# Transposes of a half's feed-forward output made between the next half's key projection tiles, in place of behind them

## The chip, the cores and the metric

The kernel runs on one core of one Trainium2 chip, as a single program. The metric is the device time of one execution in microseconds (us), taken as the median of several runs; lower is better. The engines are named as in the profile: PE is the matrix engine, DVE the vector engine, ACT the scalar engine, POOL the general-purpose engine and SP the engine that issues most DMAs. Each runs its own queue of instructions in order and waits for the others on semaphores.

## The reference

Three blocks follow each other, in float32, for 4 batches of 576 positions:

```python
scores = scale * np.matmul(q, k.transpose(0, 1, 3, 2))        # 8 heads of 64
thresh = np.max(scores, axis=-1, keepdims=True) - tau
attn   = softmax of the scores that reach thresh;  x = attn @ v
xk = mu_k * x + (1.0 - mu_k) * x_prev                         # x_prev: x one position earlier
xr = mu_r * x + (1.0 - mu_r) * x_prev
k = np.maximum(xk @ w_k, 0.0)                                 # 512 -> 1024
v = k * k @ w_v                                               # 1024 -> 512
x = 1.0 / (1.0 + np.exp(-(xr @ w_r))) * v
u = x + real(fft over positions and channels of x)
un = layer norm of u;  out = u + np.maximum(un @ w_ch1, 0.0) @ w_ch2
```

The change touches the second block, the feed-forward, alone.

## The kernel before, in words

The attention of the 16 pairs of heads is cut into 144 steps. From the fifth pair on, the feed-forward runs beside it as a stream: a Python generator, `ffn_stream`, that emits a piece of work, yields its cost and is resumed as attention steps leave credit. What the stream has left when attention ends runs in a second stage, beside the Fourier transform (`fft_fold`, `fft_one`, `fft_two`, on tiles `f`, `fz`, `fa`, `fb`), the first norms (`un`, `ut`) and the conversion of the last block's weights (`wbits`, `cA`, `cB`). The last block (tiles `c1ps`, `c2ps`) follows.

The stream walks over 4 batches with 2 halves of 288 positions each. A half consists of

- K: eight key projection tiles `kps`, 12 matmuls each. ACT evicts each (`relu`, its square, a copy) and POOL makes a low part;
- R: four tiles `rps` of 12 matmuls from `xh`, `xl` and `wr`, evicted by ACT with a tanh into the tile `tg`;
- V: four tiles `vps` of 24 matmuls, which DVE multiplies into `tg`;
- the output, `xt_out`: three tiles `xn` (128, 128 and 32 positions). PE transposes `tg` with four instructions for each, ACT copies the result into a tile `xnat`, and ACT's DMA queue writes that to the tensor `xd`, from which the Fourier transform reads later.

A half's `xt_out` is not run at its own end. It is kept, and the next half runs it after its K and before its R. So it is run behind K in seven of the eight halves; the last half's own output comes at the very end of the stream.

Three pools matter. `kps`, `rps`, `vps`, `xn` and attention's `av` take turns in two PSUM banks (function `bank`). `xnat` has one buffer while attention runs and afterwards shares four buffers, named `o`, with `un` and other tiles. `xh` and `xl`, the operands of K, are in the second stage also the operands of R: function `build_xs` fills them anew once K has read them. While attention runs, and for the very last half, R has buffers of its own and is prepared during K.

The order on each engine is made by a scheduler that plans the emitted instructions by costs of its own. It keeps what each must wait for, but may move work of one part past work of another, so the order written in the kernel is not the one on the engine.

Of the kernel before, what the change touches and what calls it, by code (L numbers as in the profile page):

```python
# [1 line left out]

# [1 line left out]

# [24 lines left out]
def tile_kernel(ctx: ExitStack, tc: tile.TileContext, a):  # L29
# [87 lines left out]
    def bank(shape, name):  # L117
        if psm is None:
            if P['AVR'] == 0:
                return pst.tile(shape, F32, tag="t", name=name)  # L120
            if not avq:
                t = pss.tile([128, 2, 512], F32, tag="s", name="avs")
                avq.extend([t[:, 0, 0:HS], t[:, 1, 0:HS]])
            return avq.pop(0)
        while len(pending) >= 2:
            pending.pop(0)()
        return psm.tile(shape, F32, tag="m", name=name)
# [3 lines left out]
    def settle():  # L131
        go, second[:] = list(second), []
        for f in go:
            f()
        while pending:
            pending.pop(0)()
# [262 lines left out]
    def proj(ps, w, x, m, width, nk):  # L399
        for k in range(nk):  # L400
            wh, wl = (t_[:, k * width + 128 * m:k * width + 128 * m + 128] for t_ in w)
            pe.matmul(ps, wh, x[0][k], start=(k == 0), stop=False)  # L402
            pe.matmul(ps, wh, x[1][k], start=False, stop=False)  # L403
            pe.matmul(ps, wl, x[0][k], start=False, stop=(k == nk - 1))  # L404
# [37 lines left out]
    def ffn_stream():  # L442
        fp = ffn["pool"]
        xt_out = None
        for b in range(B):
            for half in range(2):
                if half == 0:
                    while xdone[P['XH'] == 0] < NPAIR * (b + 1):
                        yield 0
                    xs = build_xs(b, half, 0)  # L450
                while builds:
                    yield 0
                xs_r = build_xs(b, half, 1) if state['at'] or (b, half) == (B - 1, 1) else None
                k2 = [fp.tile([128, 8, HS], F32R, tag=f"k2{i}", name=f"k2{i}") for i in range(2)]
                for f in range(8):
                    ps = bank([128, HS], "kps")
                    proj(ps, wk[f // 4], xs, f % 4, 512, 4)

                    def post(f=f, ps=ps, k2=k2, b=b):
                        r = fp.tile([128, HS], F32, tag="relu", bufs=2, name="relu")  # L460
                        m = P['RQ'][f]
                        if m in (1, 4):
                            dve.tensor_scalar(r, ps, 0.0, None, op0=ALU.max)
                        else:
                            with tc.high_priority(offset=400 if last else 0):
                                act.activation(r, ps, AF.Relu)
                        if m == 2:
                            pool.tensor_tensor(r, r, r, op=ALU.mult)
                        elif m == 5:
                            dve.tensor_tensor(r, r, r, op=ALU.mult)  # L470
                        elif m not in (1, 3):
                            act.activation(r, r, AF.Square)

                        def post2():
                            if m in (1, 3):
                                act.activation(k2[0][:, f, :], r, AF.Square)
                                pool.tensor_tensor(r, r, r, op=ALU.mult)
                            else:
                                act.activation(k2[0][:, f, :], r, AF.Copy)
                            eng = dve if b == B - 1 and f % 4 < P['K2'] else pool  # L480
                            eng.tensor_tensor(k2[1][:, f, :], r, k2[0][:, f, :].bitcast(F32), op=ALU.subtract)

                        second.append(post2)

                    pending.append(post)
                    if f == 3 and (b, half) == (B - 1, 1):
                        ffn["k_done"] = 1
                    yield 1.48
                if b == B - 1 and half == 1:
                    ffn["k_done"] = 2  # L490
                xs_r = xs_r or build_xs(b, half, 1)
                if xt_out:
                    yield from xt_out()
                while builds:
                    yield 0
                if half == 0:
                    while xdone[1] < NPAIR * (b + 1):
                        yield 0
                    xs = build_xs(b, 1, 0)
                for _ in state['late']:  # L500
                    pass
                t = fp.tile([128, 4, HS], F32, tag="t", name="tg")
                for m in range(4):
                    ps = bank([128, HS], "rps")
                    proj(ps, wr, xs_r, m, D, 4)

                    def post(m=m, ps=ps, half=half, t=t):
                        o = t[:, m, ::-1] if half else t[:, m, :]
                        with tc.high_priority(offset=400 if last else 0):
                            act.activation(o, ps, AF.Tanh, scale=0.5)  # L510

                    pending.append(post)
                    yield 1.48
                settle()
                settle()
                if b == B - 1 and half == 1:
                    ffn["r_done"] = True
                for m in range(4):
                    ps = bank([128, HS], "vps")
                    for k in range(8):  # L520
                        c = k * D + 128 * m
                        pe.matmul(ps, wv[0][:, c:c + 128], k2[0][:, k, :], start=(k == 0), stop=False)  # L522
                        pe.matmul(ps, wv[0][:, c:c + 128], k2[1][:, k, :], start=False, stop=False)  # L523
                        pe.matmul(ps, wv[1][:, c:c + 128], k2[0][:, k, :], start=False, stop=(k == 7))  # L524

                    def post(m=m, ps=ps, half=half, t=t):
                        v = ps[:, ::-1] if half else ps
                        with tc.high_priority(offset=400 if last else 0):
                            dve.scalar_tensor_tensor(t[:, m, :], t[:, m, :], 1.0, v, op0=ALU.add, op1=ALU.mult)  # L529

                    pending.append(post)
                    yield 2.95

                def xt_out(b=b, half=half, t=t):
                    settle()
                    for t0 in (0, 128, 256):
                        tn = min(128, HS - t0)
                        ps = bank([128, D], "xn")
                        for m in range(4):
                            pe.transpose(ps[:tn, 128 * m:128 * (m + 1)], t[:, m, t0:t0 + tn], ident)  # L540

                        def post(t0=t0, tn=tn, ps=ps):
                            n = fp.tile([128, D], F32, tag="xn", name="xnat") if last is None else last.tile([128, D], F32, tag="o", bufs=4, name="xnat")
                            if P['XN'] >> (t0 // 128) & 1:
                                dve.tensor_scalar(n[:tn], ps[:tn], 0.5, None, op0=ALU.mult)
                            else:
                                with tc.high_priority(offset=400 if last else 0):
                                    act.activation(n[:tn], ps[:tn], AF.Copy, scale=0.5)
                            r0 = half * (HS + 1) + t0
                            act.dma_start(xd[b][r0:r0 + tn, :], n[:tn])  # L550
                            if half and t0 == 256:
                                act.dma_start(xd[b][HS:HS + 1, :], n[tn - 1:tn])

                        pending.append(post)
                        yield 0.45
                    written[b] += 1

        yield from xt_out()
# [653 lines left out]
```

## Time and profile before

| | us |
|---|---|
| median of 3 runs | 1078.95 |
| lowest, highest | 1077.89, 1082.51 |
| the profiled execution | 1083.47 |
| its span, first to last instruction | 1081.7 |
| PE busy in the span | 1019.9 |

The span lies 1.8 us inside the profiled execution's own time, and that execution is 4.5 us above the median. The stretches that matter are attention with the stream (to about 522 us), the second stage (to about 641 us) and the last block (to the end). An `xn` group begins at 227.7, 297.9, 365.7, 434.5, 503.3, 554.6 and 603.5 us, and the last one, which stays where it is, at 636.8 us.

### The profile page before, as it was taken

To read this page: it belongs to the slowest core of one execution; us is meant where nothing else is said; L and a number is where in the kernel's file an instruction comes from. 1 tells how busy PE (TensorE), PEld (TensorE's weight loads), DVE (VectorE), ACT (ScalarE), POOL (GpSimd) and SP (SyncE) were. 2 spreads that over 40 slices of the span, in tenths; PEclk is the share of its full clock that TensorE was granted. 3 is DMA by queue.
4 is the path that set the end of the run, shared out by engine and by line. 5 is a ranking of instruction groups with operands and counts; after the bars stand their busy time and mean duration, and the time that the engine had idled before them with its cause. 6 is when DMAs were issued, how large, how long until landed. Compare 5 with 4: busy or idle time off the path is not lost.

```text
span 1081.7 us, 18932 instructions
## 1 busy us (share of the span) xinstructions
PE 1019.9 (94%) x6933; PEld 897.4 (83%) x6933; DVE 671.7 (62%) x1797; ACT 518.0 (48%) x1211; POOL 367.8 (34%) x472
## 2 busy tenths in 40 slices
PE   5888889999999999999999899999999999999998
PEld 4555668988889889888899789898898898999997
DVE  6889888667686675765357878556448465222322
ACT  4768676585776757757165645233223122111111
POOL 1555777455673554734233100000014133010000
PEclk9989889999999999999999899999999999999999
DMA  6432421111122111200623565535336435232221
GB/s 233 148 112 75 133 90 59 37 58 59 60 69 60 58 37 60 69 14 23 185 65 103 175 201 183 160 111 193 121 114 187 152 128 174 78 103 93 98 98 59
DMA packets 45526, 114.54 MB, mean 106 GB/s; under 512 B 6208, under 2 KB 6629, under 8 KB 45433
## 3 DMA queue, kind: packets, MB, share of 16 engines
q1 hardware_dynamic: 27920, 74.43, 21.3%
q10 hardware_dynamic: 12200, 22.17, 6.7%
q0 software_dynamic: 5312, 16.72, 4.3%
q8 instruction: 55, 0.90, 0.3%
q14 instruction: 39, 0.31, 0.1%
HBM read 84.98 MB, written 28.32 MB: 105 GB/s over the span
## 4 chain that ended last, share of the span: by engine, by line
PE 65%; DVE 10%; DMA 6%; ACT 5%; issue 3%; POOL 3%; ACTq 0%; DVEq 0%; SPq 0%
PE av L382 5%; PE c1ps L971 5%; PE c1ps L972 5%; PE c1ps L973 5%; PE c2ps L984 5%; PE c2ps L986 5%; PE c2ps L985 5%; PE s L221 4%; DMA wraw<-in_w_ch 3%; PE t L323 3%; PE kps L402 2%; PE kps L404 2%; PE kps L403 2%; PE vps L522 2%; PE vps L523 2%
## 5 line engine op out<-in xcount | busy, mean ns | idle before, releaser
L977 DVE SCALAR_TENSOR_TENSOR hl<-c1ps,hh 128x256 fp32r<-128x256 f32 x144 | 60.7, 422 | 172.5 <-ACT hh L976 172.2
L976 ACT ACTIVATE hh<-c1ps 128x256 fp32r<-128x256 f32 x144 | 55.0, 382 | 224.5 <-PE c1ps L973 221.1
L261 DVE TENSOR_REDUCE small<-s 128x1 f32<-128x576 f32 x144 | 106.8, 752 | 53.7 <-PE s L221 40.4
L1009 POOL DMA_DIRECT2D ud<-u x54 | 29.5, 546 | 288.1 <-DVE u L1008 256.9
L284 POOL TENSOR_SCALAR e<-e,small 128x576 f32<-128x576 f32 x112 | 92.2, 828 | 100.1 <-DVE small L629 84.8
L276 DVE SCALAR_TENSOR_TENSOR e<-s,small,e 128x576 f32<-128x576 f32 x128 | 102.7, 812 | 25.0 <-ACT e L272 23.5
L272 ACT ACTIVATE e<-s,small 128x576 f32<-128x576 f32 x128 | 93.4, 743 | 32.1 <-DVE small L261 29.7
L323 PE MATMUL t<-ident,e 128*128 128x128 f32 x512 | 81.8, 277 | 10.5 <-POOL e L284 3.3
L326 ACT ACTIVATE pt<-t 128x512 f32<-128x512 f32 x128 | 74.6, 599 | 24.7 <-PE t L323 24.4
L971 PE MATMUL c1ps<-ut,cA 128*128 128x256 f32 x288 | 81.7, 284 | 2.9 <-ACT ut L962 1.8
L971 PE MATMUL c1ps<-ut,cB 128*128 128x256 f32 x288 | 81.2, 282 | 0.0
L972 PE MATMUL c1ps<-ut,cA 128*128 128x256 f32 x288 | 81.2, 282 | 0.0
L972 PE MATMUL c1ps<-ut,cB 128*128 128x256 f32 x288 | 81.0, 281 | 0.0
L973 PE MATMUL c1ps<-ut,cA 128*128 128x256 f32 x288 | 81.0, 281 | 0.0
L973 PE MATMUL c1ps<-ut,cB 128*128 128x256 f32 x288 | 80.9, 281 | 0.0
L402 PE MATMUL kps<-xh,wk 128*128 128x288 f32 x256 | 78.8, 308 | 1.5 <-DVE tg L529 1.2
L323 PEld LDWEIGHTS t<-ident,e 128*128 128x128 f32 x512 | 61.1, 142 | 21.0 <-POOL e L284 6.2
L404 PE MATMUL kps<-xh,wk 128*128 128x288 f32 x256 | 77.2, 302 | 0.0
L403 PE MATMUL kps<-xl,wk 128*128 128x288 f32 x256 | 77.1, 301 | 0.0
L522 PE MATMUL vps<-k,wv 128*128 128x288 f32 x256 | 76.8, 305 | 0.0
L523 PE MATMUL vps<-k,wv 128*128 128x288 f32 x256 | 76.4, 302 | 0.0
L524 PE MATMUL vps<-k,wv 128*128 128x288 f32 x256 | 75.4, 300 | 0.0
(246 smaller groups left out, 3041.4 us busy)
## 6 DMA issues: line engine op xcount, KB each, us to landing
u<-ud SPq DMA_DIRECT2D x36, 512.0 KB, 5.7
wraw<-in_w_ch ACTq DMA_DIRECT2D x64, 256.0 KB, 3.1
rawqk<-in_qk SPq DMA_DIRECT2D x24, 608.0 KB, 3.8
ud<-u POOLq DMA_DIRECT2D x54, 256.0 KB, 2.5
v<-in_v SPq DMA_DIRECT2D x16, 320.0 KB, 3.0
un<-ud SPq DMA_DIRECT2D x18, 256.0 KB, 3.6
out<-u SPq DMA_DIRECT2D x18, 256.0 KB, 2.1
wraw<-in_w_k SPq DMA_DIRECT2D x8, 512.0 KB, 3.9
```

Of the source, the lines that this page charges most:

```text
L261: dve.tensor_reduce(st[:, 0:1], sps[n][:, :, 0:HS], axis=AX.XY, op=ALU.max, negate=True)
L272: act.activation(two(eview(n)), sps[n][:, :, 0:HS], AF.Exp, bias=st[:, 0:1])
L276: dve.scalar_tensor_tensor(e, sps[n][:, :, 0:HS], st[:, 1:2], e, op0=ALU.is_ge, op1=ALU.mult, accum_out=st[:, 2:3])
L323: pe.transpose(t[:, k, :], e[:, o + 128 * k:o + 128 * (k + 1)], ident)
L402: pe.matmul(ps, wh, x[0][k], start=(k == 0), stop=False)
L403: pe.matmul(ps, wh, x[1][k], start=False, stop=False)
L404: pe.matmul(ps, wl, x[0][k], start=False, stop=(k == nk - 1))
L522: pe.matmul(ps, wv[0][:, c:c + 128], k2[0][:, k, :], start=(k == 0), stop=False)
L523: pe.matmul(ps, wv[0][:, c:c + 128], k2[1][:, k, :], start=False, stop=False)
L971: pe.matmul(ps, wh, ut[0][:, k, :], start=(k == 0), stop=False)
L972: pe.matmul(ps, wh, ut[1][:, k, :], start=False, stop=False)
L973: pe.matmul(ps, wl, ut[0][:, k, :], start=False, stop=(k == 3))
```

## The change

The generator that makes the three `xn` tiles is created before K. One of its tiles is taken after each of K's tiles 1, 3 and 5 (counted from 0); what is left of it runs after K. The call between K and R is gone.

```diff
+from itertools import islice
...
                 xs_r = build_xs(b, half, 1) if state['at'] or (b, half) == (B - 1, 1) else None
+                turned = xt_out() if xt_out else iter(())
...
                     yield 1.48
+                    if f in (1, 3, 5):
+                        yield from islice(turned, 1)
+                yield from turned
                 if b == B - 1 and half == 1:
                     ffn["k_done"] = 2
                 xs_r = xs_r or build_xs(b, half, 1)
-                if xt_out:
-                    yield from xt_out()
                 while builds:
                     yield 0
```

The number of instructions on each engine is the same before and after, kind by kind. Source lines are higher by 1 to 5 in the changed kernel.

On PE, where K of the half in the stretch from 434 us ends, with attention's scores (`s`) and transposes (`t`, `tm`) around it, the kernel before has:

```order
L404 MATMUL kps_5066<-xh_4676,wk11_87 128x288
L221 MATMUL s_5148<-kh_4800,q_4804 128x288 x2
L221 MATMUL s_5148<-kl_4801,q_4804 128x288 x2
L540 MATMUL xn_5084<-ident_76,tg_4251 128x128 x4
L221 MATMUL s_5210<-kh_4544,q_4635 128x288 x2
L221 MATMUL s_5210<-kl_4545,q_4635 128x288 x2
L540 MATMUL xn_5089<-ident_76,tg_4251 128x128 x4
L540 MATMUL xn_5124<-ident_76,tg_4251 32x128 x4
L343 MATMUL tm_5225<-ident_76,em_5097 128x128 x4
```

The three `xn` tiles stand in a row there, with R behind them. In the changed kernel PE passes from the last K tile of the same half (`kps_5091`) to R without anything between:

```order
L404 MATMUL kps_5091<-xl_4677,wk10_86 128x288
L405 MATMUL kps_5091<-xh_4676,wk11_87 128x288
L403 MATMUL rps_5134<-xh_4742,wr0_90 128x288
L404 MATMUL rps_5134<-xl_4743,wr0_90 128x288
L405 MATMUL rps_5134<-xh_4742,wr1_91 128x288
```

The `xn` tiles have moved up between K tiles. The first of them now stands on PE between K's second tile (`kps_4759`) and its third (`kps_4830`):

```order
L405 MATMUL kps_4759<-xh_4676,wk01_85 128x288
L324 MATMUL t_4815<-ident_76,e_4679 128x128 x4
L324 MATMUL t_4873<-ident_76,e_4679 128x128 x4
L543 MATMUL xn_4778<-ident_76,tg_4249 128x128 x4
L222 MATMUL s_4907<-kh_4795,q_4799 128x288 x2
L222 MATMUL s_4907<-kl_4796,q_4799 128x288 x2
L403 MATMUL kps_4830<-xh_4676,wk00_84 128x288
```

Of the 21 moved tiles 20 have other work of attention or of the transform beside them in this way. One has not: the second of the half that follows attention stands directly between two K tiles.

On PE, in that half (the `xn` group at 554.6 us), the kernel before comes from K through 5.6 us of transform and `xn` work, and then to R, tile after tile:

```order
L811 MATMUL fz_6676<-tc2_6213,G1_6523 1x258
L820 MATMUL fb_6694<-ts2_6214,H1_6525 128x256
L402 MATMUL rps_6648<-xh_6564,wr0_90 128x288
L403 MATMUL rps_6648<-xl_6565,wr0_90 128x288
L404 MATMUL rps_6648<-xh_6564,wr1_91 128x288
```

In the changed kernel 16 transform matmuls are left between K's last tile and R (7 of `f`, 3 of `fb`, 6 of `fz`), and PE makes the first two R tiles (`rps_6691`, `rps_6741`) in turns:

```order
L814 MATMUL fz_6639<-tc2_6213,G1_6500 1x258
L823 MATMUL fb_6657<-ts2_6214,H1_6502 128x256
L403 MATMUL rps_6691<-xh_6623,wr0_90 128x288
L403 MATMUL rps_6741<-xh_6623,wr0_90 128x288
L404 MATMUL rps_6691<-xl_6624,wr0_90 128x288
L405 MATMUL rps_6691<-xh_6623,wr1_91 128x288
```

After 12 matmuls of R come 7 of the transform (`fz`, `fb`), two of R, 7 of `fa`, six of R and 7 of `fa`; the rest of R follows.

On ACT, in the last half (the `xn` group at 603.5 us), the kernel before evicts the three `xn` tiles together, between steps of the transform (`fee`, `fdd`):

```order
L834 ACTIVATE fee_7475<-zr_7457 1x257
L548 ACTIVATE xnat_7267<-xn_7239 128x512
L833 ACTIVATE fdd_7474<-zr_7457 1x257
L550 DMA xd3_66<-xnat_7267 128x512
L548 ACTIVATE xnat_7270<-xn_7262 128x512
L548 ACTIVATE xnat_7348<-xn_7313 32x512
```

The changed kernel evicts the first two among K's tiles, and the third (`xnat_7248`) behind K's last one (`kps_7284`):

```order
L468 ACTIVATE relu_7300<-kps_7284 128x288
L55 DMA wraw_7353<-in_w_ch2 128x512
L551 ACTIVATE xnat_7248<-xn_7239 32x512
L474 ACTIVATE relu_7300<-relu_7300 128x288
L553 DMA xd3_66<-xnat_7248 32x512
```

So that tile keeps one of the two PSUM banks from its four transposes, in front of K's seventh tile, to the end of K. K's last two tiles and R's first share the other, with 7 transform matmuls before K's seventh, 13 before its eighth and four transposes `ut` before R's first.

## Rows read from the trace of the kernel before

**Rows 1.** The page's parts 1 and 2: busy us, then 40 slices.

```profile
PE 1019.9 (94%) x6933; PEld 897.4 (83%) x6933; DVE 671.7 (62%) x1797; ACT 518.0 (48%) x1211; POOL 367.8 (34%) x472
...
PEclk9989889999999999999999899999999999999999
```

**Rows 2.** Busy time by stretch: us, then PE, PEld, DVE, ACT, POOL, PEclk, DMA, GB/s.

```profile
226.00:240.00 14.00, 13.66 (x108) 11.97 (x108) 8.47 (x26) 11.74 (x27) 7.56 (x11) 1.00 0.20 67
240.00:297.00 57.00, 56.82 (x439) 51.13 (x439) 40.77 (x113) 37.59 (x85) 32.21 (x41) 1.00 0.18 57
297.00:311.00 14.00, 11.83 (x86) 10.24 (x86) 12.14 (x30) 12.17 (x29) 10.60 (x15) 1.00 0.25 83
365.00:374.00 9.00, 8.10 (x58) 6.98 (x58) 7.97 (x22) 7.70 (x16) 6.07 (x8) 1.00 0.28 96
374.00:434.00 60.00, 59.30 (x461) 53.62 (x460) 40.43 (x118) 39.03 (x88) 30.78 (x40) 1.00 0.18 55
434.00:446.00 12.00, 10.03 (x72) 8.58 (x71) 9.71 (x25) 9.27 (x23) 11.78 (x16) 1.00 0.31 96
503.00:511.00 8.00, 6.52 (x52) 5.80 (x51) 6.12 (x16) 6.96 (x19) 4.50 (x7) 1.00 0.18 67
```

**Rows 3.** PE in order of time, behind two K stages: start, us, what, [idle <-releaser].

```profile
436.40 0.61 PE L540 MATMUL xn<-ident,tg 128*32 128x128 f32 x4 [0.33 <-ACT xnat L548]
437.74 0.66 PE L343 MATMUL tm<-ident,em 128*128 128x128 f32 x4 [0.72 <-POOL em L284]
...
439.77 0.41 PE L402 MATMUL rps<-xh,wr 128*128 128x288 f32 x1 [0.50 <-ACT xnat L548]
...
442.42 0.52 PE L221 MATMUL s<-kh,q 128*128 128x288 f32 x2 [0.35 <-DVE e L276]
...
508.38 0.40 PE L402 MATMUL rps<-xh,wr 128*128 128x288 f32 x1 [0.79 <-ACT xnat L548]
```

**Rows 4.** ACT in order of time, 434 to 446 us: the third eviction.

```profile
445.21 0.59 ACT L548 ACTIVATE xnat<-xn 32x512 f32<-32x512 f32 x1 [1.87 <-DMA xd<-xnat]
```

**Rows 5.** Busy time by stretch in the last half: columns as in Rows 2.

```profile
603.00:624.00 21.00, 16.75 (x96) 14.29 (x97) 18.05 (x53) 12.67 (x32) 1.90 (x3) 0.84 0.72 239
612.00:616.00 4.00, 2.65 (x12) 1.97 (x13) 3.97 (x13) 1.62 (x4) 0.00 (x0) 0.66 0.67 247
616.00:620.00 4.00, 4.00 (x19) 4.00 (x18) 1.98 (x7) 2.69 (x5) 0.00 (x0) 0.50 1.01 319
```

**Rows 6.** PE in order of time, 603 to 616 us.

```profile
605.61 0.66 PE L540 MATMUL xn<-ident,tg 128*128 128x128 f32 x4 [1.22 <-ACT relu L466]
...
612.05 0.61 PE L540 MATMUL xn<-ident,tg 128*32 128x128 f32 x4 [0.69 <-ACT xnat L548]
...
615.03 0.61 PE L402 MATMUL rps<-xr,wr 128*128 128x288 f32 x1 [0.69 <-ACT xnat L548]
```

**Rows 7.** ACT in order of time, 603 to 616 us.

```profile
611.40 0.60 ACT L548 ACTIVATE xnat<-xn 128x512 f32<-128x512 f32 x1
...
614.38 0.60 ACT L548 ACTIVATE xnat<-xn 128x512 f32<-128x512 f32 x1 [2.09 <-PE ut L959]
```

**Rows 8.** PE in order of time: K's end and R's start after attention.

```profile
553.36 0.29 PE L403 MATMUL kps<-xl,wk 128*128 128x288 f32 x1
553.49 0.30 PE L404 MATMUL kps<-xh,wk 128*128 128x288 f32 x1
...
559.21 0.30 PE L402 MATMUL rps<-xh,wr 128*128 128x288 f32 x1
```

**Rows 9.** ACT in order of time, same place: R's operand, chunks 1, 2 and 4.

```profile
554.20 0.77 ACT L433 ACTIVATE xh<-xtmp 128x288 fp32r<-128x288 f32 x2
...
557.76 0.44 ACT L433 ACTIVATE xh<-xtmp 128x288 fp32r<-128x288 f32 x1
```

**Rows 10.** DVE in order of time, same place: low part of chunk 3.

```profile
557.91 0.44 DVE L435 TENSOR_TENSOR xl<-xtmp,xh 128x288 fp32r<-128x288 f32 x1
```

**Rows 11.** POOL in order of time, same place: low part of chunk 4.

```profile
558.93 0.81 POOL L435 TENSOR_TENSOR xl<-xtmp,xh 128x288 fp32r<-128x288 f32 x1
```

## The prediction, made before the changed kernel was run

> **What bounds the kernel now.** I read the page first. PE is busy for 1019.9 of 1081.7 us, DVE for 671.7, the others for less, and PE's granted clock is near full in all but four slices [rows 1]. So PE sets the time. What a change can win is PE's waiting and the work that PE does at a lower clock, and the question is where these lie.
>
> The busy times by stretch answer it. Between the `xn` groups PE hardly waits: 0.18 us in the 57 from 240 to 297, 0.70 in the 60 from 374 to 434. Behind a K stage it does: stretch less busy time gives 0.34 + 2.17 + 0.90 + 1.97 + 1.48 = 6.86 us in the five stretches of attention that begin with an `xn` group [rows 2]. The last half is worse. From 603 to 624 us PE is idle for 21.00 - 16.75 = 4.25 us, and the granted clock falls to 0.66 and then 0.50, which is the lower of its two levels, 1.2 in place of 2.4 GHz [rows 5].
>
> PE's order of time shows why. The third `xn` group and R's first tiles wait for ACT to evict an `xn` tile (0.33, 0.50 and 0.79 us), since three `xn` tiles and R share two banks, and in the same places PE waits for POOL's `em` and DVE's `e` (0.72, 0.35), because with R held back it has only attention's own chain to run [rows 3]. ACT is late for a reason of its own: with one `xnat` buffer an eviction waits for the DMA of the one before it, 1.87 us in the third eviction [rows 4]. In the last half, `xn` tiles made at 603.5 and 605.6 us are evicted at 611.40 and 614.38, the second waiting 2.09 us for `ut` transposes, as `un` holds the shared buffers [rows 7]; R cannot begin before 615.03 [rows 6].
>
> **The change part by part.** No instruction is added or removed. The 84 transposes, 21 evictions and 24 DMAs of seven outputs move forward past six, four and two K tiles of the next half (for the three tiles of an output). Their own time on PE stays the same. So the sum consists of waits.
>
> *Attention, five halves.* At the end of K nothing of `xn` stands before R any more, so the waits on `xnat` end, and K and R tiles stand ready beside attention's chain throughout. An eviction now has two K tiles, that is 24 matmuls 0.13 us apart [rows 8] and attention's work between them, 3.1 us at least, from the one before in which the DMA before it can land. At most all 6.86 us go; at least none, if PE meets the same waits for `e` and `em` elsewhere. I take three quarters, 5.1 us, because almost all of PE's waiting from 240 to 511 us is in these places, and in the stretches where K tiles stand ready beside attention it is 0.18 and 0.70 us [rows 2].
>
> *The last half.* Two of its `xn` tiles are evicted before `un` takes the buffers, so both banks are not blocked, and transform and `ut` run beside K. At stake are the 4.25 us of waiting and the loss by the clock: from 616 to 620 us four busy microseconds at 0.50 do the work of two, so 2.0, and from 612 to 616 us 2.65 busy at 0.66 lose 0.9 [rows 5]. Together 7.15 us. I take three quarters again, 5.3 us, because DVE, whose transform steps PE also waited for, is busy for 18.05 of these 21 us [rows 5]; the bounds are 0 and 7.15.
>
> *New: tiles that PE waits behind.* Where an `xn` tile stands between two K tiles, the second of them uses the bank of the tile right before the `xn`, and must wait for its `relu`. In 20 of 21 places some work stands beside it. One is bare, and in the last half K's last two tiles and R's first share one bank, with 7, 13 and 4 instructions in front of them. PE's waits for an eviction run from 0.33 to 1.22 us [rows 3, 6]; the nearest, in attention, are 0.33, 0.50 and 0.79 [rows 3]. Two at about 0.5 make 1.0 us. The bounds are 0 and, with six at 0.5, 3.0.
>
> *New: R's operand after attention.* In the first half behind attention `xh` and `xl` of R go into the buffers that K has just read. Before, this was covered: K ends at 553.49 + 0.13 = 553.62, R begins at 559.21 [rows 8], and PE had 5.6 us of transposes and transform in between. The refill takes longer than that: its first chunks are written at 554.20, the last at 557.76 [rows 9], and the low parts of chunks 3 and 4 end at 557.91 + 0.44 = 558.35 and 558.93 + 0.81 = 559.74 [rows 10, 11], 4.7 and 6.1 us behind K. Now 16 matmuls stand there, about 2.1 us at 0.13. Then 12 of R with the first two chunks (1.6), and 7 of the transform (0.9): that makes 4.6 us, when chunk 3 is about ready; two of R and seven more of the transform reach 5.8, against 6.1 for chunk 4. I take 0.8 us of waiting for these two and for the delays between them. Nothing is lost if the refill is quicker, as three evictions of about 0.6 us leave its place on ACT; if the transform waits too, 6.1 - 2.1 - 1.6 = 2.4.
>
> *Queues.* ACT's DMA issues move with the evictions, and the weight loads for the last block in the same queue come a little later: nine of the sixteen first weight pieces may only start when K is over, which was ahead of the three `xn` steps of the last half and is now behind them. DVE has 2.95 idle microseconds even from 603 to 624 us [rows 5] and the pieces are not read before the last block, so I count nothing; if DVE's backlog is still there when the last block starts, part of the gain of the last half is paid back there.
>
> *Sum.* 5.1 + 5.3 - 1.0 - 0.8 = 8.6 us less. The profiled execution would come to 1083.47 - 8.6 = 1074.9 us. It lay 4.5 us above the median of the runs, 1078.95, and a wait of PE is the same in either, so the median becomes 1078.95 - 8.6 = 1070.4 us.
>
> A page weighs against the change: the Trainium skill, "TensorE: Matmul & The Clock Gate", section "A second HAM failure mode: psum-queue depth-cycling", tells of a kernel whose matrix engine pauses briefly between groups as it goes round its PSUM banks, with the clock falling and rising again. By that, more turns over two banks would be dearer than their waits. The trace agrees where both banks were blocked [rows 5, 6]; in the attention stretches it does not, for there the same short waits left the clock at 1.00 [rows 2].
>
> **The rivals.** *The waits only move* (chance 0.17). PE's waits for `e` and `em` belong to attention's chain, and K and R work used up earlier is missing later. For it: two of the five waits shown are of this kind [rows 3]. Against it: PE is free of waits wherever K or R tiles stand ready [rows 2]. Attention then gives 0, and 5.3 - 1.0 - 0.8 = 3.5: 1075.5 us.
>
> *The clock falls in K* (0.10). The bank waits and the refill lower the clock in the two halves after attention, as from 612 to 620 us, at 2.9 us a time. 8.6 - 2 x 2.9 = 2.8: 1076.2 us. This is what the page's rule would do here.
>
> *Slower: every moved tile exposes an eviction* (0.14). The tile behind an `xn` waits for the `relu` of the tile before, on an ACT queue in which `xnat` may itself stand waiting for its DMA, as for 1.87 us in [rows 4]. The six waits for an eviction in rows 3 and 6 (0.33, 0.50, 0.79, 1.22, 0.69, 0.69) have a mean of 0.70 us; 21 times that is 14.8 us in place of my 1.0, so 5.1 + 5.3 - 14.8 - 0.8 = -5.2: 1084.2 us. It decides from (5.1 + 5.3 - 0.8) / 21 = 0.46 us a tile. Against it: 20 of 21 tiles have other work beside them.
>
> *All waits go* (0.12). 6.86 + 7.15 = 14.0, nothing new: 1065.0 us.
>
> **How the numbers follow.** The forecast has 0.47; its own range is 1067 to 1075 us (either share between a half and nearly all, the new waits between 0 and 3). The time is its time, 1070.4. Half a per cent, 5.4 us, is what a measurement of this kernel can tell from no change, so faster means below 1073.6 and slower above 1084.3. Faster: 0.38 of the forecast's 0.47, all of the 0.12 and 0.05 of the moved waits and the clock: 0.55. Slower: a good half of the exposed evictions, 0.08, and 0.04 for what I don't see in a schedule rearranged from 200 us on: 0.12. The rest, 0.33, is the same. The range for eight times in ten is 1064 to 1083.
>
> **What would show it.** In the profile after, the stretches behind K in attention should hold under 2 us of PE's waiting in all, with no PE wait on `xnat`; R of the last half should follow K at full clock, and no slice near 600 us show 8. R's first tiles behind attention should wait for `xl` or `xh` for about 0.8 us, and PE for `relu` in front of a few K tiles. The prediction is wrong if PE's waiting from 220 to 511 us is as large as before in other places, if `relu` waits turn up in front of many K tiles, or if PE waits longer than before for weights or `ut` when the last block starts.

## The result, and the profile after

The changed kernel takes 1062.82 us (median of 6 runs, 1059.58 to 1066.76) beside 1078.42 for the kernel before (6 runs, 1076.95 to 1082.51), so 15.6 us less by the medians. The ratio, estimated from the single runs, is 0.9844, 95% interval 0.9822 to 0.9866, or 16.8 us less (14.5 to 19.2). Forecast were 1070.4 us and a range from 1064 to 1083, so the gain is almost twice the forecast's 8.6 us and the time lies just below the range. A second timing of the same kernel, among the last experiments, gave a ratio of 0.9869 (0.9839 to 0.9899), or 14.1 us less.

Of the page of the kernel after, parts 1 and 2, which answer to [rows 1]:

```profile
PE 1009.4 (95%) x6933; PEld 891.7 (84%) x6933; DVE 675.0 (64%) x1797; ACT 520.6 (49%) x1211; POOL 368.7 (35%) x472
...
PEclk9999889999999999999999999999999999999999
```

The instructions are the same in number. The slice from 595 to 622 us, which showed an 8, now shows a 9; two slices between 106 and 160 us still show 8, as they did. The one from 53 to 80 us went from 8 to 9 as well, but no moved tile stands there, so that is not the change's doing. PE's busy time fell by 10.5 us without an instruction less, to which I come back.

Busy time by stretch of the kernel after, columns as in [rows 2]: five stretches as long as those of [rows 2] that began with an `xn` group, each ending shortly behind R's start, and two of four microseconds that answer to [rows 5].

```profile
228.00:242.00 14.00, 14.00 (x109) 12.60 (x108) 10.27 (x28) 11.42 (x28) 9.88 (x13) 1.00 0.16 49
294.00:308.00 14.00, 14.00 (x109) 12.60 (x109) 9.87 (x27) 10.87 (x25) 8.88 (x12) 1.00 0.24 73
361.00:370.00 9.00, 8.95 (x71) 7.88 (x68) 6.18 (x17) 7.15 (x19) 5.45 (x8) 1.00 0.31 96
425.00:437.00 12.00, 12.00 (x95) 11.95 (x95) 9.59 (x26) 11.00 (x28) 8.24 (x10) 1.00 0.18 58
491.00:499.00 8.00, 8.00 (x64) 8.00 (x63) 6.00 (x16) 7.34 (x19) 3.45 (x5) 1.00 0.04 8
596.00:600.00 4.00, 3.28 (x24) 3.28 (x25) 4.00 (x13) 3.62 (x8) 1.47 (x1) 1.00 0.82 279
600.00:604.00 4.00, 3.79 (x30) 3.56 (x28) 3.63 (x13) 2.85 (x6) 0.00 (x0) 1.00 0.66 220
```

The 6.86 us of waiting behind K have become 0.05, and R of the last half runs at full clock.

To set the two executions side by side, I take two stretches that hold the same work in either: from the first K tile of the first batch's second half to the first K tile behind attention, and from there to the first `c1ps` of the last block. PE alone, of the kernel before (us, busy and count, PEclk, DMA, GB/s):

```profile
203.68:534.17 330.49, 321.64 (x2450) 1.00 0.18 57
534.17:640.95 106.78, 96.42 (x663) 0.95 0.43 131
```

And of the kernel after:

```profile
202.93:523.25 320.32, 318.47 (x2449) 1.00 0.18 59
523.25:622.11 98.86, 91.80 (x663) 1.00 0.44 137
```

Beside attention 10.2 us went, behind it 7.9. In the first stretch the reader sees two things fall: the idle time, from 330.49 - 321.64 = 8.85 to 1.85 us, and the busy time of the same matmuls, by 3.2 us. Behind attention the busy time fell by 4.6 us. There the kernel before has the lower clock of [rows 5] and one more such place, behind a wait of 1.85 us for `fseh`, which [rows 5] do not show (PE alone):

```profile
541.00:546.00 5.00, 4.64 (x23) 0.66 0.22 62
```

In the kernel after neither is left. The spans differ by 20.3 us, more than the medians do, since the profiled execution of the kernel before lay 5 us above its median; 2.2 us of it lie ahead of these two stretches and behind them. The experiments, which are timed, say how much of it belongs to each stretch.

What PE waits for in the kernel after, in order of time (start, us, what, [idle <-releaser]), which answers to [rows 3, 6, 8]:

```profile
528.94 0.66 PE L543 MATMUL xn<-ident,tg 128*128 128x128 f32 x4 [0.66 <-ACT relu L468]
...
545.12 0.29 PE L405 MATMUL kps<-xh,wk 128*128 128x288 f32 x1
...
554.38 0.40 PE L403 MATMUL rps<-xh,wr 128*128 128x288 f32 x1 [0.24 <-ACT tg L513]
...
596.72 0.40 PE L403 MATMUL rps<-xr,wr 128*128 128x288 f32 x1 [0.93 <-ACT relu L468]
...
619.03 0.76 PE L543 MATMUL xn<-ident,tg 128*128 128x128 f32 x5 [1.36 <-DVE tg L532]
...
622.11 0.48 PE L974 MATMUL c1ps<-ut,cA 128*128 128x256 f32 x1 [1.45 <-ACT ut L965]
```

No wait on `xnat` is left beside K or R. Waits on `relu` are more: with 0.35 us at 278.40 and 0.23 at 589.98 there are four of them, 2.17 us, where the kernel before had two, 1.38 us (0.16 at 216.95 and the 1.22 of [rows 6]). Just ahead of the last block stand 1.36 us for `tg` and 1.45 for `ut`, together 2.81 us, where the kernel before waited 0.22 for `tg`, 0.25 for `xnat` and 1.78 for `ut`, together 2.25 us.

ACT's evictions in the last half of the kernel after, where [rows 7] had the first at 611.40 and a wait of 2.09 us before the second:

```profile
583.34 0.58 ACT L551 ACTIVATE xnat<-xn 128x512 f32<-128x512 f32 x1
...
596.58 0.57 ACT L551 ACTIVATE xnat<-xn 32x512 f32<-32x512 f32 x1
```

### The profile page after: what moved, and what is told of

It is laid out like the page before. It is cut to its first block, busy times and chain, and to the rows that moved or that the text cites. A ratio compares the mean times of both kernels' runs of the same rounds, so it can differ in the third digit from the quotient of the medians.

```text
span 1061.4 us, 18937 instructions
## 1 busy us (share of the span) xinstructions
PE 1009.4 (95%) x6933; PEld 891.7 (84%) x6933; DVE 675.0 (64%) x1797; ACT 520.6 (49%) x1211; POOL 368.7 (35%) x472
## 4 chain that ended last, share of the span: by engine, by line
PE 67%; DVE 10%; DMA 6%; POOL 3%; issue 2%; ACT 2%; SPq 0%; DVEq 0%; ACTq 0%; POOLq 0%
PE av L383 6%; PE c1ps L974 6%; PE c1ps L975 6%; PE c1ps L976 6%; PE c2ps L987 5%; PE c2ps L989 5%; PE c2ps L988 5%; PE s L222 4%; PE t L324 3%; PE kps L403 2%; PE kps L405 2%; PE kps L404 2%; DMA wraw<-in_w_ch 2%; PE vps L526 2%; PE vps L525 2%
## 5 line engine op out<-in xcount | busy, mean ns | idle before, releaser
L324 PE MATMUL t<-ident,e 128*128 128x128 f32 x512 | 79.3, 276 | 11.0 <-ACT e L638 3.3
```

The source lines that it names most:

```text
L324: pe.transpose(t[:, k, :], e[:, o + 128 * k:o + 128 * (k + 1)], ident)
```

## The experiments

Differences in us are the ratio's, at 1079 us. The experiments were timed on four chips, each beside the kernel before on its own chip. The two timings of the changed kernel differ by 0.0025, so I take variants on different chips to be told apart from about 3 us on, an estimate.

| kernel | ratio to before, 95% | us |
|---|---|---|
| moved only beside attention | 0.9896 (0.9872, 0.9920) | -11.2 |
| moved only behind attention | 0.9959 (0.9943, 0.9975) | -4.4 |
| all three in a row behind K tile 3 | 0.9897 (0.9878, 0.9915) | -11.1 |
| behind K tiles 2, 4, 6 | 0.9868 (0.9850, 0.9887) | -14.2 |
| one moved, behind K tile 3 | 1.0005 (0.9986, 1.0025) | +0.5 |
| one moved, behind K tile 1 | 0.9973 (0.9954, 0.9991) | -2.9 |
| two moved, behind K tiles 2, 5 | 0.9867 (0.9846, 0.9888) | -14.4 |
| before, space freed (control) | 0.9978 (0.9959, 0.9997) | -2.4 |
| before, two `xnat` tiles beside attention | 0.9913 (0.9898, 0.9929) | -9.4 |
| before, idle tile for `xnat` behind attention | 0.9972 (0.9953, 0.9991) | -3.0 |
| after, low parts on GpSimd | 0.9878 (0.9846, 0.9910) | -13.2 |
| after, space freed (control) | 0.9882 (0.9860, 0.9904) | -12.7 |
| after, two `xnat` tiles beside attention | 0.9891 (0.9869, 0.9914) | -11.8 |
| after, again | 0.9869 (0.9839, 0.9899) | -14.1 |

**Each part of the change alone.**

```diff
+                early = b < B - 1          # the other kernel: b == B - 1
-                    if f in (1, 3, 5):
+                    if early and f in (1, 3, 5):
 ...
-                yield from turned
+                if early:
+                    yield from turned
 ...
+                yield from turned
```

> Only the five halves beside the attention have their three transpose tiles between K tiles; in the two halves behind the attention they stand behind K as before. Theory A, that the stretch between K and R itself blocks TensorE (the three tiles and R's first tile follow each other through two banks, and around each wait short restarts are lost that the profile does not list as idle): the attention part of the gain comes whole, about 10 us, so 1067 to 1070 us, and the last half still shows its gaps of 603 to 624 us in the kernel before. Rival B, that the idle time as listed is all there is to gain there (6.9 us at most, 5.1 as predicted): 1072 to 1074 us. Rival C, that the gain comes from the instruction order shifting by chance somewhere: the two parts do not add up to the whole 16 us.

> The counterpart: only the two halves behind the attention have their transpose tiles between K tiles. Theory A: the last half gains what the two profiles show between its first K tile and its first V tile, 7.9 us, and gives 1.2 back before the last block, and the half before it gains 1.2; so -6 to -8 us, 1070 to 1072 us. Rival B, the sizes as predicted (5.3 less 0.8 for R's operands): 1074 us. Rival C: the saving of this kernel and that of the kernel with the attention part alone do not add up to 16 us within 2 us.

The parts add up, 11.2 + 4.4 = 15.6 us, between the 14.1 and 16.8 of the two timings of the whole, so rival C does not hold. The part beside attention is as theory A had it. The part behind it is 4.4 us (2.7 to 6.1), less than theory A's 6 to 8 and what rival B gave. The profiled execution of the kernel before had exaggerated that stretch: the kernel with the attention part alone has nearly the order of before there, and needs 105.30 us at a mean clock of 0.98 where the kernel before needed 106.78 at 0.95. The two stretches, of the kernel with the attention part alone:

```profile
206.23:526.30 320.07, 318.30 (x2450) 1.00 0.18 59
526.30:631.60 105.30, 94.33 (x663) 0.98 0.44 132
```

and of the kernel with the late part alone:

```profile
202.75:533.33 330.58, 321.62 (x2450) 1.00 0.18 58
533.33:632.42 99.09, 91.12 (x663) 1.00 0.45 136
```

Each stretch is short exactly where its tiles were moved (320.07 as after, 330.58 as before), and PE's busy time falls with it.

**Place or spacing.**

```diff
-                    if f in (1, 3, 5):
-                        yield from islice(turned, 1)
+                    if f == 3:
+                        yield from turned
```

> All three tiles stand in one row behind K tile 3, in every half: away from the border of K and R, but not apart from each other. If the place decides (R's first tile and the build of R's operands behind the transposes), the time is that of the changed kernel, 1063 us within 2. If the spacing decides (each tile waits for the eviction of the one before it, whose SBUF tile has its DMA to land first), the waits come back inside K: 3 tiles and K tile 4 in a chain, and the time is 1070 to 1077 us. Theory A, with both at work, expects 1067 to 1071 us, and idle TensorE time before xn and kps tiles that the eviction xnat ends.

Both, as theory A expected. Its stretch beside attention and two of the waits that came back there:

```profile
204.45:529.49 325.04, 318.67 (x2450) 1.00 0.18 58
```

```profile
217.89 0.66 PE L543 MATMUL xn<-ident,tg 128*128 128x128 f32 x4 [1.50 <-ACT relu L468]
...
345.45 0.40 PE L403 MATMUL kps<-xh,wk 128*128 128x288 f32 x1 [1.16 <-ACT relu L468]
```

A row of three inside K costs 325.04 - 320.32 = 4.7 us against three apart in the profiles. By the timings, on different chips, it is 3.0 or 5.7 us, by which timing of the changed kernel is taken; the smaller is at the edge of what can be told. PE waits for `relu`, not for `xnat` as I had written.

**Other places apart.** The tuple (1, 3, 5) became (2, 4, 6).

> As the changed kernel, but with the tiles behind K tiles 2, 4 and 6 in place of 1, 3 and 5. Theory A (the border is free of transposes, the tiles stand apart): the same as the changed kernel, 1063 us within 2. Theory D, phase: the credit that a half spends up to its R is the same, so the border falls on the same steps and the time is the same too, within 3 us; only a collision of a single tile with a step would tell, and then by under 1 us a half. If it comes out above 1068 us, neither holds, and the places 1, 3 and 5 were lucky ones.

The ratio lies between those of the changed kernel's two timings, so 1, 3 and 5 are no lucky places.

**How many tiles may stay at the border.** One moved (behind K tile 3, then behind tile 1), then two, the rest behind K as before:

```diff
-                    if f in (1, 3, 5):
+                    if f == 3:             # then f == 1, then f in (2, 5)
                         yield from islice(turned, 1)
-                yield from turned
 ...
                 xs_r = xs_r or build_xs(b, half, 1)
+                yield from turned
```

> Only one of the three tiles of a half is moved (behind K tile 3); the other two stay behind K, so the chain between K and R is one tile shorter. If the chain is what costs, a third to a half of the 16 us goes: 1070 to 1074 us. If any tile at the border blocks as much as three (the wait is R's for a bank and for its operands), next to nothing is gained: 1076 to 1079 us. If the third tile in the chain alone waits (because the one SBUF tile is held by the DMA of the second), nearly all goes: 1063 to 1067 us.

> One of three tiles moved, as in the kernel that gained nothing, but behind K tile 1 in place of 3. Theory A' (two tiles that are left between K and R wait for each other's DMA as much as three): again no gain, 1077 to 1081 us. Theory D (the kernel with the one tile behind K tile 3 ran into a collision at the border: VectorE had the operands of the next half and the conversion of q before the e that the score tiles wait for): the gain of 4 to 8 us that one tile less in the chain brings shows here, 1070 to 1075 us.

> Two of the three tiles of a half are moved (behind K tiles 2 and 5), the last stays behind K. With none moved the time is 1078.8 us, with one 1079.5, with all three 1062.8. Theory A, a chain of tiles between K and R: the chain is now one tile long, so most of the 16 us goes: 1066 to 1070 us. Theory D, that what costs is where the border of K and R falls among the steps of the attention (the two tensor engines' helpers, VectorE and GpSimd, are loaded there with the operands of the next half and the heads of the next pair, and the score tiles of TensorE queue behind that): the time depends on the phase and not on the number of tiles: anything from 1063 to 1080 us, and TensorE's waits at the border are for e, em and xtmp rather than for xnat.

Beside attention nearly nothing is gained with two tiles left at the border, and most of it with one left: it is the second tile there that costs. That stretch takes 322.87 us with one left and 329.24 with two left and the first behind K tile 1. Of the kernel with two left and the first behind K tile 3 it is:

```profile
202.36:536.43 334.07, 322.50 (x2449) 0.99 0.17 57
```

Its longest wait there, on PE:

```profile
375.74 0.82 PE L222 MATMUL s<-kh,q 128*128 128x288 f32 x2 [2.76 <-DVE e L277]
```

and what DVE did meanwhile:

```profile
371.80 0.99 DVE L433 SCALAR_TENSOR_TENSOR xtmp<-xt,small,xtmp 128x288 f32<-128x288 f32 x1
372.83 1.91 DVE L191 SCALAR_TENSOR_TENSOR q<-rawqk,small,q 64x640 fp32r<-64x640 f32 x1
374.77 0.82 DVE L277 SCALAR_TENSOR_TENSOR e<-s,small,e 128x576 f32<-128x576 f32 x1
```

The `e` that PE needs stands behind an `xtmp` and a `q`, and R stands behind the score tile in PE's queue. Such a wait cost more than its length here. The granted clock fell at this border and at one more, where PE had waited 0.85 and then 1.65 us (PE alone):

```profile
306.00:311.00 5.00, 4.12 (x21) 0.66 0.43 138
374.00:379.00 5.00, 3.26 (x15) 0.66 0.44 138
```

A mean clock of 0.66 over five microseconds takes 1.7 us of full speed, so the two places cost up to 3.4 us, an estimate. That is most of the 334.07 - 330.49 = 3.6 us by which this stretch is longer than in the kernel before. The kernel with the tile behind K tile 1 shows 1.00 over its stretch. Behind attention both gain: 100.50 and 102.35 us in place of 106.78, so the +0.5 of the table is a loss beside attention set against a gain behind it.

My collision theory expected that the kernel with the tile behind K tile 3 was unlucky and that the place behind K tile 1 would gain 4 to 8 us. It gained 2.9 (1.0 to 5.0), and had the same kind of waits. So the collision is a part of what two tiles at the border do, and of the two kernels only the first has the fall of the clock beside attention; why the order comes out so is not settled.

**The single SBUF tile of xnat.** The control gives up one of two buffers `xtmp` and one of five `w`; the other kernel uses the space.

```diff
-  n = fp.tile([128, D], F32, tag="xn", name="xnat") if last is None else ...
+  n = fp.tile([128, D], F32, tag="xn", bufs=2, name="xnat") if last is None else ...
 ...
```

> The kernel before with one buffer in place of two for the products xtmp in the build of the operands, and four in place of five for the temporaries of the Fourier step (tag w). It is there as the kernel that the next one is compared with, which needs that space. All theories: 1078 to 1083 us.

> As the kernel with the freed space, and two SBUF tiles in place of one for the evicted transposes of the halves beside the attention, so that an eviction need not wait until the DMA of the one before it has landed. The order of the instructions stays that of the kernel before. If the single tile is what costs in the attention (the prediction's reading: xnat waits for the DMA, and TensorE for xnat, 0.33 + 0.50 + 0.79 us where it is listed), 3 to 8 us go against the kernel with the freed space. Theory A (banks and order between K and R): 1 to 2 us go. Theory D, phase: within 1 us, for no step moves.

The buffer is shared with the conversion of `w_v`, so that has two as well; it is over by 160 us. With no tile moved, the second buffer is worth 9.4 - 2.4 = 7.0 us (4.4 to 9.7 by the two intervals, an estimate). ACT's evictions at the second border, of the kernel before:

```profile
299.98 0.62 ACT L548 ACTIVATE xnat<-xn 128x512 f32<-128x512 f32 x1
...
303.48 0.68 ACT L548 ACTIVATE xnat<-xn 128x512 f32<-128x512 f32 x1
...
307.87 0.57 ACT L548 ACTIVATE xnat<-xn 32x512 f32<-32x512 f32 x1
```

and of the kernel with two buffers:

```profile
300.99 0.62 ACT L548 ACTIVATE xnat<-xn 128x512 f32<-128x512 f32 x1
...
302.28 0.64 ACT L548 ACTIVATE xnat<-xn 128x512 f32<-128x512 f32 x1
...
306.12 0.57 ACT L548 ACTIVATE xnat<-xn 32x512 f32<-32x512 f32 x1
```

The second follows the first by 1.3 us in place of 3.5. Over the five borders beside attention no two evictions in a row start less than 2.85 us apart in the kernel before; with two buffers seven of ten do. An eviction takes 0.6 us and its DMA 2.0 us (median, 1.6 at the least) from issue to landing, so one buffer explains such a spacing. Before, no idle time is written at 303.48, for ACT did other work in between: the eviction's late place is in the order, and the trace names no wait for the DMA there. Theory A had expected only 1 to 2 us and is off on that point. The stretch of the kernel with two buffers, 6.2 us shorter than before:

```profile
204.98:529.32 324.34, 319.18 (x2455) 1.00 0.18 58
```

Two things keep me from calling all of the 7.0 us the wait for the DMA. PE's written waits for `xnat` ahead of R beside attention are 2.2 us in the control and 2.1 with two buffers, so the gain is not in them. And the scheduler orders the two kernels differently from about 150 us on, and the control's profiled execution has the lower clock at two of the borders (PE alone), where the kernel with two buffers has 1.00:

```profile
301.00:306.00 5.00, 3.98 (x21) 0.66 0.55 175
444.00:449.00 5.00, 4.67 (x24) 0.66 0.47 141
```

These two places cost up to 3.4 us, the same estimate as above.

The same two kernels on the changed order tell whether buffer and place are one loss:

> The changed kernel with the two SBUF tiles for xnat beside the attention (and the two buffers given up that make room for them). In the order of before the second tile was worth 6.3 us. If the second buffer and the new places remove the same waits (the chain of tiles between K and R, each behind the DMA of the one before it), it is worth nothing here: the same as the changed kernel with the freed space alone, within 2 us. If the two are losses of their own, it is 4 to 6 us faster.

> The changed kernel with one buffer for xtmp and four for the temporaries w, as control for the kernel with two xnat tiles. Before the change these buffers made 2.4 us (0.2%) less. If that carries over: 1060 to 1061 us, else as the changed kernel, 1063 us.

> The changed kernel itself, beside the two that vary it. All theories: 0.984 of the kernel before within 0.003, and in its trace nearly no listed wait of TensorE between 220 and 520 us.

0.9891 against 0.9882: with the tiles apart, the second buffer is worth nothing that can be told (between 4.4 us slower and 2.4 faster, by the two intervals). So what the buffer cures the spacing cures as well, and the spacing, at 11.2 against 7.0 us, seems to cure more. The control's own 2.4 us did not carry over.

**The shared buffers behind attention.**

```diff
-  ... if last is None else last.tile(... tag="o", bufs=4 ...)
+  ... if last is None or ((b, half) != (B - 1, 1) and t0 != 128) else last.tile(... tag="o", bufs=4 ...)
```

> The kernel before, but the first and third transpose tile of the halves behind the attention are evicted into the SBUF tile that the halves beside the attention used and that lies idle then; only the second goes into the four buffers that it shares with the normalised rows un. The order stays that of before. The part of the change behind the attention was worth 4.65 us by itself. If the buffers held by un are what delays those evictions (the prediction's reading), 2 to 4 us go: 1075 to 1077 us, the waits of 0.69 us on xnat at 612 and 615 us are gone. If the clock or the order is what costs there, 0 to 1 us goes: 1078 to 1080 us.

3.0 us (1.0 to 5.1) of the 4.4 go with the written order unchanged; the scheduler's plan behind attention is another one, and evicts the third tile second. Busy time by stretch where [rows 5] had clocks of 0.66 and 0.50:

```profile
612.00:616.00 4.00, 4.00 (x33) 4.00 (x33) 3.02 (x10) 1.43 (x4) 0.00 (x0) 1.00 0.85 277
616.00:620.00 4.00, 4.00 (x33) 4.00 (x32) 3.09 (x10) 1.25 (x3) 0.00 (x0) 1.00 0.88 250
```

The first two evictions of the last half come at 601.91 and 606.22 us and R starts at 607.84, where the kernel before had 611.40, 614.38 and 615.03 [rows 6, 7]. So the buffers held by `un` delayed the evictions, R was blocked, and the clock fell with it.

**What is paid back ahead of the last block.**

```diff
-        ... lows=dve if q < 2 else None)
+        ... lows=dve if q == 1 else None)
```

> The changed kernel, with the low parts of the first quarter of the last block's weights computed by GpSimd (idle from 604 us on) in place of VectorE. If the 1.36 us that the last transposes wait for tg, and what follows it, come from VectorE's backlog (35 of 38 us busy up to 622 us), 1 to 3 us go: 1060 to 1062 us, and the wait before the last xn is under 0.5 us. If GpSimd's slower subtraction holds the weights up, or VectorE runs slower beside a busy GpSimd, it is as much slower: 1064 to 1068 us.

The wait for `tg` grew. Of this kernel, first PE in order of time:

```profile
624.17 0.76 PE L543 MATMUL xn<-ident,tg 128*128 128x128 f32 x5 [2.23 <-DVE tg L532]
```

then POOL by line from 604 to 627 us (busy us and mean ns, then idle us before and what ended it):

```profile
L76 POOL TENSOR_TENSOR cA<-wbits,cA 128x256 fp32r<-128x256 f32 x8 | 7.4, 939 | 13.9 <-ACT cA L73 13.9
```

and DVE's line that waits for it:

```profile
L68 DVE TENSOR_SCALAR wbits<-wraw 128x256 int32<-128x256 int32 x9 | 3.6, 402 | 4.7 <-POOL cA L76 3.8 <-DMA wraw<-in_w_ch 0.9
```

In the kernel after, the same lines, on DVE, from 604 to 622 us:

```profile
L76 DVE TENSOR_TENSOR cA<-wbits,cA 128x256 fp32r<-128x256 f32 x7 | 2.9, 420 | 0.2 <-ACT cA L73 0.2
L68 DVE TENSOR_SCALAR wbits<-wraw 128x256 int32<-128x256 int32 x8 | 2.3, 290 | 1.6 <-DMA wraw<-in_w_ch 1.6
```

GpSimd takes 939 ns where VectorE takes 420, VectorE then stands 3.8 us waiting for it, and its own instruction takes 402 in place of 290 ns beside it. The stretch behind attention took 103.17 us in place of 98.86; the timed ratio, 0.9878, cannot be told from the 0.9844 and 0.9869 of the changed kernel. The Trainium skill ("Perfetto Trace Analysis", section "Optimizing Scalar/DVE Operations") warns that moving work between these two engines might not help, as they share a port; the trace agrees that it did not. That VectorE's backlog makes the 1.36 us is not shown by this, as it was not relieved.

## Why the prediction was wrong

The direction, and that PE's waits behind K are what goes, were right. The size was not, and one step carries it: "At most all 6.86 us go; at least none [...] I take three quarters, 5.1 us", which rests on "Their own time on PE stays the same. So the sum consists of waits". The part beside attention, alone, measured 11.2 us (8.6 to 13.8), and 10.4 in its profile: more than twice the term and above its upper bound.

- *The share.* Nearly all the waiting went, not three quarters. Over the whole stretch idle time fell by 7.0 us, from 8.85, with the new `relu` waits already in it. The waits for `e` and `em` that I feared would stay [rows 3] went nearly all as well (0.49 us for `e` at 216.09 and 0.15 for `em` at 394.45 are left), which fits that tiles at the border had held R back.
- *The bound.* Idle time was not all there was. PE's busy time for the same matmuls fell by 3.2 us. The rows show how. Where PE does not wait, a group is written as longer than the time until the next one starts; in the kernel after, in order of time:

```profile
405.90 1.09 PE L324 MATMUL t<-ident,e 128*128 128x128 f32 x8
406.82 0.60 PE L543 MATMUL xn<-ident,tg 128*128 128x128 f32 x4
```

The second starts 0.92 us after the first, which is written with 1.09: its last 0.17 us lie beside the next group. Where PE waits, the idle time is counted from the written end (in [rows 3], 436.40 + 0.61 + 0.72 is 437.73, the next start within 0.01), so the overlap is lost too and stands in the busy time. The stretch had 19 such waits and has 4: 15 x 0.17 = 2.6 of the 3.2 us, an estimate. The rest may be the restart: the first R matmul behind a wait is written with 0.40 and 0.41 us [rows 3] where one without has 0.30 [rows 8], up to 0.1 us a wait. The clock has no part in it, for it is 1.00 over the stretch in both kernels. The Trainium skill ("Perfetto Trace Analysis", section "Tensor Engine Instruction (MATMUL, LD_WEIGHTS)") states that the end time of a matmul in a profile is estimated and not observed; these rows agree, and starts are what to count by.
- *The reason.* "With one `xnat` buffer an eviction waits for the DMA of the one before it" was right: before, evictions start at least 2.85 us apart, and the two-buffer kernel, where they come closer, is 7.0 us faster, some of which may be the control's clock. I had read it from one written wait [rows 4] and so thought it small.

*The last half* (5.3 less its share of the new costs): the late part alone measured 4.4 us (2.7 to 6.1); 5.3 - 0.8 = 4.5. Right in size, in part by luck, since the 0.8 did not come and 0.6 us was paid back ahead of the last block. The mechanism (`un` holds the buffers, the clock falls with R) is borne out by the kernel with the idle tile, with 3.0 us.

*New waits behind `relu`*: 1.0 forecast. The profile has four waits with 2.17 us, 0.8 more than before, so the size was about right. Two stand in front of a K tile behind an `xn` (278.40 and 589.98), and one is the place foreseen, where K's last two tiles and R's first share a bank (0.93 us at 596.72).

*R's operand after attention*: 0.8 forecast, none came. K ends at 545.12 + 0.13 = 545.25. Chunk 4's low part follows it:

```profile
549.82 0.82 POOL L436 TENSOR_TENSOR xl<-xtmp,xh 128x288 fp32r<-128x288 f32 x1 [0.87 <-ACT xh L434]
```

so it is ready at 550.64, 5.4 us behind K against the 6.1 that I had taken from before. PE did the matmuls that I had counted in between and came to R's next `xl` at 551.32, 6.1 us behind K where I had 5.8. So the refill was sooner, PE a little later, and R's only wait there is 0.24 us, for `tg`.

*Queues*: counted at nothing, with the remark that DVE's backlog might take part back at the last block. PE does wait longer there, for `tg`: 2.81 us with the wait for `ut`, against 2.25 before, so 0.6 us was paid back. That the backlog is the reason is not shown.

*The rivals.* The waits did not only move. The clock did not fall in K: in the kernel after it is 1.00 over both stretches, so the rival did not come true. What the Trainium skill tells of ("TensorE: Matmul & The Clock Gate", section "A second HAM failure mode: psum-queue depth-cycling") does not show in that kernel either; the control agrees with it, for at its border at 301 us the clock fell among waits of 0.51, 0.73 and 1.02 us. Of 21 moved tiles two exposed an eviction to the K tile behind them. "All waits go", at 0.12, came nearest with 1065.0, in part by luck: it took 6.86 us beside attention where 11.2 went, and 7.15 behind it where 4.4 went.

## What to carry to other kernels

Where a small buffer makes instructions queue, look at the spacing of the instructions that share it, not only at the waits written before them: other work may fill the gap on that engine while the one that sets the time is held up. A wait of PE costs more than its idle column says, here by 3.2 us for 15 waits, and more still where the clock falls behind it, so read the granted clock of a border before explaining what a variant gained. Compare start-to-start times of the same work, or the span of a stretch with the same count. Where tiles share a buffer that drains slowly, either put other work between them or give them a second buffer; the first brought more here, and doing both bought nothing further.

## Not expected of the hardware

The overlap of 0.17 us that a wait of PE costs beyond its idle time. And a part of the wait of 2.76 us for `e` in the kernel with one tile moved: VectorE's `q` and GpSimd's `kl`, with operands of the same sizes each time, do not run side by side. At that border `kl` had started first:

```profile
372.45 1.60 POOL L168 TENSOR_TENSOR kl<-rawqk,kh 128x576 fp32r<-128x576 f32 x1
```

It ends at 374.05, and the `q` shown above, started at 372.83, ends 0.69 us behind it, after 1.91 us. At an earlier border `q` had started first:

```profile
303.49 1.01 DVE L191 SCALAR_TENSOR_TENSOR q<-rawqk,small,q 64x640 fp32r<-64x640 f32 x1
303.80 1.97 POOL L168 TENSOR_TENSOR kl<-rawqk,kh 128x576 fp32r<-128x576 f32 x1
```

Here `kl` ends 1.27 us behind `q`. In the kernel before, 17 of the 24 `q` started during a `kl`, and each ended 0.68 or 0.69 us behind it, so `q` took between 1.11 and 1.92 us; with no `kl` beside it the shortest took 0.88. So these two instructions seem to go one after the other, whichever starts first, and the one that comes second is written with the wait in its time.
